# One-hot products in place of a reload: the first 128 rows of each expert's list in a three-layer kernel

## The chip, the cores and the metric

The kernel runs on one core of one Trainium2 chip. The metric is device time in microseconds (us) of one execution, from the first to the last instruction of that core and what the device needs around them. The engines are TensorE (PE, with its weight loads PEld), VectorE (DVE), ScalarE (ACT), GpSimd (POOL) and SyncE (SP); the two memories on the core are SBUF and PSUM (the accumulators of TensorE).

## The reference

Three layers follow each other. Cut to what matters:

```python
def _attn_ref(q, k, v):                      # B=4, H=8, S=576, D=64, blocks of 64 are causal
    scores = np.matmul(q, k.transpose(0, 1, 3, 2)) / np.sqrt(64)
    scores = np.where(block_i >= block_j, scores, -1e9)
    attn = softmax(scores)                   # rows, with 1e-9 in the divisor
    return np.matmul(attn, v)

def _moe_ref(x, w_skip, w_gate, w1, w2):     # x: 2304 tokens x 512, 8 experts, hidden 1024
    do_compute = x @ w_skip > 0              # the other tokens pass unchanged
    xc = x[do_compute]
    logits = xc @ w_gate
    e_idx = np.argmax(logits, axis=1)
    gate_w = softmax(logits)[e_idx]
    for e in range(8):
        h = np.maximum(xc[e_idx == e] @ w1[e], 0.0)
        y[e_idx == e] = gate_w * (h @ w2[e])
    out[do_compute] = xc + y

def _moe2_ref(x, w_in, w_out, alpha):        # 512 -> 2048 -> 512, weights in float64
    h = x @ w_in
    g = np.maximum(h, 0.0) + alpha * np.minimum(h, 0.0)
    return (g @ w_out).astype(np.float32)
```

What each expert computes on depends on the data, so the kernel has to make, on the chip, a list of the tokens of each expert (token number and gate weight) before it can fetch their rows.

## The kernel before

**Attention** (0 to 243 us). Sixteen pairs of heads, four pairs to a batch. Each pair loads q, k and v, transposes them (`tr`, L210), splits them in two parts (`split_qk`, L223 to L227), makes five strips of scores (`sc`, L247 to L253), takes row maxima on DVE (`row_max`, L260, L263), exponents on ACT (`expo`), transposes the strips (`ptr`, L296, L298 and L311), and multiplies by v (`pv`). `xout` writes the finished rows x to the DRAM tensor `xd`. A table of offsets (`OFF`) and the framework's scheduler set the order of these instructions until the last batch; from the last steps of batch 3 on (`tc.manual_schedule()`) instructions stand as the program writes them. All transposes and the small products of the routing share three PSUM buffers (pool `ps_m`, tag `m`).

**Routing**, once for each batch b, is spread over the batch's last pair and the pair behind it: `route`, `weigh_all` and `route2` make the logits, the expert of each token and the exponents of the gate; `route3` makes the rank of each token within its expert (`rank`, five columns of 128 tokens) and the one-hot `eq` (L468: 5x32 entries a row, rank equal to 0..31). `route4` picks, through `pick` (L476, 20 small products with `eq` as weights), the token numbers of the first 32 ranks of each expert and adds them into `sli`; `route5` (L487 to L521, a chain on DVE) computes the gate `g`, the list places `pi`, and picks the gate weights into `slg`. The first 32 tokens of every expert so need no list in DRAM: their numbers are in `sid` and two gathers (`xgs`, L601) fetch their rows.

**The list.** All other tokens go through DRAM: `send` scatters (token, gate) pairs of 8 bytes into `lst` by five indirect DMAs of POOL for each batch (L506). For batch 3, `sends[B - 1]()` stands behind `s_x(0)`, and its first scatter waits for ACT's second copy there (`last_exp`, L702). Then four loads (`load_list`, L684) bring ranks 32 to 159, 160 to 287, and so on, of all experts back into SBUF as `li[0]` to `li[3]`; they wait for the scatters.

**The seam and the experts** (243 to 414 us). PE runs 13 products on constants (`warm`, L64), the last batch's gate pick, four loads of counts into registers (`load_areg`, L693), the transposes of `xgs` (`s_x`, L701), and, for the first 32 tokens of every expert, `s_one` (L717), `s_ht` (L701) and `s_two` (L733). The tokens beyond 32 come in chunks of 128 rows: `level0(e)` issues the gather of expert e's first chunk on POOL (through `li[0]`, L601; three buffers), `extra(e, ...)` runs it under a branch on the expert's count, and each chunk gathers the one behind it. `both(E, 0)` holds experts 0 and 1 under one branch (L928): it is skipped as a whole when neither has more than 32 tokens, as in the profiled run. `extra(2)` (branch L808) is the first one whose rows PE transposes (L701, `xg`). Weights of the experts stream in by `load_w` on SP (L84), a few at a time; buffers come free when an expert is done.

**The last layer** (414 us to the end) decodes its float64 weights on DVE and multiplies on PE; DVE's part lasts until about 520 us, PE's to the end.

## Time and profile before

| quantity | value |
|---|---|
| median of 3 runs | 842.71 us (842.01 to 846.03) |
| the profiled execution | 841.73 us |
| its span, first to last instruction | 840.1 us |
| PE busy in the span | 785.9 us (94%) |
| DVE, ACT, POOL busy | 459.5, 298.7, 164.6 us |
| mean granted clock of TensorE | 0.98 |

The profiled execution lies 0.98 us under the median, and 1.6 us of it lie outside the span. The page's busy shares are means over stages with different limits; the rows further below are cut by stage. Times in rows are counted from the span's start. "idle before <-releaser" is the time in which the engine stood still ahead of that group, and what the profile takes for the thing that ended it; "issue" means nothing that it shows. An engine name with a q behind it is the engine's sequencer (branches, register loads, waits).

### The profile page before, as it was taken

What the parts mean: (1) busy time and instruction counts of PE and PEld (TensorE: products, weight loads), DVE (VectorE), ACT (ScalarE), POOL (GpSimd) and SP (SyncE); (2) the same over time, 40 slices, a digit from 0 to 9 for tenths busy, and PEclk for the clock granted to TensorE, in tenths of its full rate; (3) what the DMA queues carried; (4) which work ended last, traced back from release to release, by engine and by line L of the source; (5) the groups of instructions that cost most, each with busy time, mean ns of one, the idle gap of its engine ahead of it and who ended that gap; (6) DMA issues with size and microseconds to landing.
All of it is one profiled execution on the core that took longest, in us unless ns stands there. A gap on an engine that the chain in (4) does not pass through costs nothing.

```text
span 840.1 us, 14547 instructions
## 1 busy us (share of the span) xinstructions
PE 785.9 (94%) x5553; PEld 609.5 (73%) x5553; DVE 459.5 (55%) x953; ACT 298.7 (36%) x779; POOL 164.6 (20%) x208
## 2 busy tenths in 40 slices
PE   8999999999976899897699888999999999999998
PEld 5777777777745567664588666888888888888897
DVE  5758567667549299990489898322322332222232
ACT  5776776776722122112243333211121112011211
POOL 1000200101113114213122122222222222222122
PEclk9999999999998999999799999999999999999999
DMA  7874545663317997816622230100110001000100
GB/s 142 201 207 111 139 93 132 120 167 80 95 42 210 311 305 247 315 59 203 211 94 89 76 105 22 51 0 1 51 51 1 1 26 51 0 1 1 47 5 25
DMA packets 96117, 85.77 MB, mean 102 GB/s; under 512 B 68601, under 2 KB 73913, under 8 KB 96016
## 3 DMA queue, kind: packets, MB, share of 16 engines
q1 hardware_dynamic: 92000, 77.54, 32.1%
q0 software_dynamic: 2816, 6.65, 2.5%
q8 instruction: 56, 0.92, 0.5%
q10 hardware_dynamic: 1200, 0.30, 0.2%
q14 instruction: 45, 0.37, 0.1%
HBM read 73.20 MB, written 11.71 MB: 101 GB/s over the span
## 4 chain that ended last, share of the span: by engine, by line
PE 39%; DVE 9%; issue 2%; ACT 1%; DVEq 0%; ACTq 0%
PE psf L1009 18%; PE psa L1040 6%; PE psa L1041 6%; PE psa L1050 6%; DVE dt L652 2%; DVE dr L656 1%; DVE gt L1022 1%; DVE dt L653 1%; DVE dr L654 1%; DVE dr L650 1%; DVE wkg L640 1%; DVE dt L649 1%; DVE dt L651 1%; PE psx L997 1%; DVE wlo L640 1%
## 5 line engine op out<-in xcount | busy, mean ns | idle before, releaser
L1009 PE MATMUL psf<-xs,whi 128*128 128x512 f32 (+1 forms) x640 | 158.0, 369 | 0.7 <-ACT xs L871 0.7
L1026 POOL TENSOR_TENSOR gl<-gt,gh 128x512 fp32r<-128x512 f32 (+1 forms) x80 | 96.4, 1205 | 316.2 <-ACT gh L1025 184.6
L1025 ACT ACTIVATE gh<-gt 128x512 fp32r<-128x512 f32 (+1 forms) x80 | 47.1, 589 | 263.6 <-PE psa L1041 137.8
L1009 PEld LDWEIGHTS psf<-xs,whi 128*128 128x128 f32 x640 | 114.5, 188 | 23.0 <-ACT xs L871 0.9
L1021 DVE TENSOR_SCALAR gu<-psf,alf 128x512 f32<-128x512 f32 (+1 forms) x64 | 43.7, 682 | 157.8 <-PE psf L1009 157.7
L1009 PE MATMUL psf<-xs,wlo 128*128 128x512 f32 (+1 forms) x320 | 79.3, 369 | 0.0
L277 ACT ACTIVATE pe<-pss,mx 128x512 f32<-128x512 f32 (+3 forms) x128 | 66.7, 526 | 13.6 <-DVE mx L260 12.1
L1009 PEld LDWEIGHTS psf<-xs,wlo 128*128 128x128 f32 x320 | 56.8, 188 | 10.3
L1040 PE MATMUL psa<-whi,gh 128*128 128x512 f32 x144 | 57.3, 398 | 6.8 <-ACT gh L1025 6.8
L285 ACT ACTIVATE pt<-pspt 128x512 f32<-128x512 f32 (+3 forms) x112 | 51.8, 488 | 30.7 <-PE pspt L311 30.0
L1040 PE MATMUL psa<-wkg,gh 128*128 128x512 f32 x144 | 57.0, 396 | 1.6 <-ACT gh L1025 1.6
L260 DVE TENSOR_REDUCE mx<-pss 128x2 f32<-128x1024 f32 (+1 forms) x64 | 52.3, 818 | 10.9 <-PE pss L249 10.7
L1022 DVE SCALAR_TENSOR_TENSOR gt<-psf,gu 128x512 f32<-128x512 f32 (+1 forms) x80 | 51.0, 637 | 11.6 <-POOL gl L1026 5.0
L1041 PE MATMUL psa<-wlo,gh 128*128 128x512 f32 x144 | 56.2, 390 | 0.0
L1041 PE MATMUL psa<-wkg,gh 128*128 128x512 f32 x144 | 56.2, 390 | 0.0
L311 PE MATMUL pspt<-ident,pe 128*128 128x128 f32 x320 | 51.0, 286 | 0.5 <-ACT pt L397 0.3
L336 PE MATMUL pso<-pt,vr 128*64 128x256 f32 (+1 forms) x384 | 47.1, 352 | 3.7 <-ACT pt L285 3.6
L872 DVE TENSOR_TENSOR xs<-psx,xs 128x512 fp32r<-128x512 f32 x18 | 12.5, 692 | 57.4 <-ACT xs L871 57.4
L336 PEld LDWEIGHTS pso<-pt,vr 128*64 128x64 f32 x384 | 29.8, 136 | 18.0 <-ACT pt L285 8.4
L766 PEld LDWEIGHTS psh<-xT,w1t 128*128 128x128 f32 x320 | 39.9, 207 | 1.9 <-issue 1.0
L766 PE MATMUL psh<-xT,w1t 128*128 128x128 f32 x320 | 40.7, 292 | 0.1
L311 PEld LDWEIGHTS pspt<-ident,pe 128*128 128x128 f32 x320 | 33.6, 141 | 7.5 <-issue 2.2
(233 smaller groups left out, 1351.6 us busy)
## 6 DMA issues: line engine op xcount, KB each, us to landing
w1t<-in_moe_w_dram SPq DMA_DIRECT2D x32, 512.0 KB, 6.1
w2t<-in_moe_w_dram SPq DMA_DIRECT2D x32, 512.0 KB, 5.3
dr<-in_moe_w_in_dram SPq DMA_DIRECT2D x16, 512.0 KB, 5.8
dr<-in_moe_w_out_dram SPq DMA_DIRECT2D x16, 512.0 KB, 3.6
out_dram<-ob SPq DMA_DIRECT2D x18, 256.0 KB, 2.0
qr<-in_q_dram SPq DMA_DIRECT2D x32, 128.0 KB, 4.0
vr<-in_v_dram SPq DMA_DIRECT2D x32, 128.0 KB, 2.6
kr<-in_k_dram SPq DMA_DIRECT2D x30, 128.0 KB, 4.7
```

What stands on the lines that cost most here:

```text
L260: nc.vector.tensor_reduce(out=m, in_=ps[:, :, 0:128 * i + 128], axis=AX.X, op=ALU.max, negate=True)
L277: ins = nc.scalar.activation(out=pt[:, x, 0:n], in_=ps[:, x, 0:n], func=AF.Exp, bias=m[:, x:x + 1], scale=1.0, accum_out=d["sum"][:, x * 4 ...
L285: nc.scalar.activation(out=o, in_=a, func=AF.Copy)
L311: nc.tensor.transpose(ps[:, y, j, :], e[:, x, j * 128:j * 128 + 128], ident)
L336: nc.tensor.matmul(d["o"][hs, c0:c0 + n * 128], v5[:, j, x, :], pt[:, x, 2 * j:2 * j + n].rearrange("p n c -> p (n c)"), start=(j == 0), s ...
L766: nc.tensor.matmul(ps[:, f], w[:, kk, c:c + 128], self.xT[:, kk], start=(kk == 0), stop=(kk == 3))
L1009: nc.tensor.matmul(ps[:, 0:n], wsp[f // 4 * 4 + kk][a][:, ws], c[:, kk, 0:n], start=(n0 == 0 and kk == 0), stop=(n0 == 2 and kk == 3))
L1022: nc.vector.scalar_tensor_tensor(out=t[:, 0:n], in0=ps[:, 0:n], scalar=0.0, in1=u[:, 0:n], op0=ALU.max, op1=ALU.add)
L1026: nc.gpsimd.tensor_tensor(out=lo[:, 0:n], in0=t[:, 0:n], in1=hi[:, 0:n].bitcast(F32), op=ALU.subtract)
L1040: nc.tensor.matmul(o, hi[:, ts], whi, start=(f == 0), stop=False)
L1041: nc.tensor.matmul(o, hi[:, ts], wlo, start=False, stop=False)
L1050: nc.tensor.matmul(acc[w, t], lo[:, t * 128:t * 128 + 128], whi, start=False, stop=False)
```

## The change

For the first 128 list rows of each expert (ranks 32 to 159, what `li[0]` held) the list is made in SBUF in the way that the first 32 ranks already are. `first_eq` makes a second one-hot `eqf` (5x128 entries a row: rank equal to 32..159); `first_pick` multiplies it with `ohi` (token numbers) and later with `ohg` (gates), five products each, and adds the result on DVE into `fli` and `flg`. For batches 0 to 2 this runs inside `route4` and `route5`, in the attention. For the last batch the token pick stands behind the two `xgs` gathers and ahead of `route5`. The tile `first` takes the place of `li[0]`, one list load is gone, and `level0(0)` to `level0(2)` stand ahead of `sends[B - 1]`, of the weight loads that are tied to it, and of the remaining three list loads.

```diff
+    iot32 = acst.tile([128, 128], BF16, name="iot32")
+    nc.vector.tensor_scalar(out=iot32, in0=iot, scalar1=32.0, scalar2=None, op0=ALU.add)
+    first = const.tile([128, E, 2], I32, name="first")
+    fli = acst.tile([128, E, 2], F32, name="fli")
+    nc.vector.memset(fli[:, :, 0], float(PADROW))
+    nc.vector.memset(fli[:, :, 1], 0.0)
+    flg = acst.tile([128, E, 3], F32, name="flg")
+    nc.vector.memset(flg, 0.0)
...
+    def first_eq(b):
+        eq = T5("eqf", 128, BF16)
+        nc.vector.tensor_tensor(out=eq, in0=iot32.unsqueeze(1).to_broadcast([128, 5, 128]), in1=rs[b][4].to_broadcast([128, 5, 128]), op=ALU.is_equal)
+        rs[b].append(eq)
+
+    def first_pick(b, src, n, acc):
+        ps = ps_m.tile([128, E, n], F32, tag="m", name="psl")
+        for t in range(5):
+            nc.tensor.matmul(ps, rs[b][6][:, t], src[:, t], start=(t == 0), stop=(t == 4))
+        nc.vector.tensor_tensor(out=acc, in0=acc, in1=ps, op=ALU.add)
+
+    def first_ids(b):
+        first_eq(b)
+        first_pick(b, rs[b][1], 2, fli)
+
     def route4(b):
         nc.vector.tensor_tensor(out=sli, in0=sli, in1=pick(b, rs[b][1], 2), op=ALU.add)
+        if b < B - 1:
+            first_ids(b)
...
         nc.vector.tensor_tensor(out=slg, in0=slg, in1=pick(b, ohg, 3), op=ALU.add)
+        first_pick(b, ohg, 3, flg)
...
     gather(xgs[1], sid[:, 1:2])
+    first_ids(B - 1)
+    nc.vector.tensor_tensor(out=first[:, :, 0], in0=fli[:, :, 0], in1=fli[:, :, 1], op=ALU.add)
     route5(B - 1)
+    nc.vector.tensor_reduce(out=first[:, :, 1].bitcast(F32), in_=flg, axis=AX.X, op=ALU.add)
...
-    li = [mw.tile([128, E, 2], I32, tag=f"li{i}", name="li", bufs=1) for i in range(KX)]
+    li = [first] + [mw.tile([128, E, 2], I32, tag=f"li{i}", name="li", bufs=1) for i in range(1, KX)]
...
     s_x(0)
-    sends[B - 1]()
-    tied[0] = last_exp[0]
-    load_w(2, range(4, 8))
-    for i in range(KX):
-        load_list(i)
...
-    level0(0)
-    level0(1)
-    level0(2)
+    for e in range(3):
+        level0(e)
+    sends[B - 1]()
+    tied[0] = last_exp[0]
+    load_w(2, range(4, 8))
+    for i in range(1, KX):
+        load_list(i)
     s_one(0)
```

What that does to the order is shown at three places. A row is one instruction with its line, its output and inputs; line numbers of the kernel after are its own, some 8 to 30 higher. `x4` folds equal rows; "..." stands for further pairs of the same kind.

**The seam, PE.** Before, behind the last batch's token pick (`eq`, L476), the count product (L595) and the 13 products on `ones`, comes the gate pick:

```order
L476 MATMUL psl<-ohi,eq 32x4
L595 LDWEIGHTS ones
L595 MATMUL psl<-run_cnt,ones 128x8
L64 MATMUL psw<-ones 128x512
...
L476 LDWEIGHTS eq
L476 MATMUL psl<-ohg,eq 32x6
...
L693 TENSOR_LOAD cnt x4
L701 MATMUL pst<-ident,xgs 128x128 x4
```

After, in the same place:

```order
L484 MATMUL psl<-ohi,eq 32x4
L621 MATMUL psl<-run_cnt,ones 128x8
L64 MATMUL psw<-ones 128x512
...
L495 LDWEIGHTS eqf
L495 MATMUL psl<-ohi,eqf 128x16
...
L484 MATMUL psl<-ohg,eq 32x6
...
L495 MATMUL psl<-ohg,eqf 128x24
...
L722 TENSOR_LOAD cnt x4
L730 MATMUL pst<-ident,xgs 128x128 x4
```

Five products for the token numbers now stand behind the 13 on `ones`, and five for the gates behind the gate pick.

**The seam, DVE.** Before, `route5`'s chain follows the counts at once:

```order
L590 TENSOR_TENSOR sid<-sli 128x2
L592 CAST sidf<-sid 128x1
L596 CAST cnt<-psl 128x8
L598 TENSOR_TENSOR cnt<-cnt 128x1 x2
L487 TENSOR_REDUCE g<-ex 128x5
L488 TENSOR_SCALAR g<-g 128x5
```

After:

```order
L616 TENSOR_TENSOR sid<-sli 128x2
L618 CAST sidf<-sid 128x1
L622 CAST cnt<-psl 128x8
L624 TENSOR_TENSOR cnt<-cnt 128x1 x2
L489 TENSOR_TENSOR eqf<-iot_113,rank 128x640
L496 TENSOR_TENSOR fli<-fli,psl 128x16
L638 TENSOR_TENSOR first<-fli 128x8
L512 TENSOR_REDUCE g<-ex 128x5
```

The addition into `fli` reads PE's five products, and all of `route5`'s chain stands behind it.

**The seam, POOL.** Before, the scatters of batch 3 stand ahead of the gathers through `li` (a one-element memset, `pad`, stands between every two):

```order
L601 DMA xgs<-xd,sid 128x512
L693 TENSOR_LOAD cnt x4
L506 DMA lst<-pr,pi 19456x2
...
L69 MEMSET pad 1x1
L601 DMA xg<-xd,li 128x512
```

After:

```order
L627 DMA xgs<-xd,sid 128x512
L722 TENSOR_LOAD cnt x4
L69 MEMSET pad 1x1
L627 DMA xg<-xd,first 128x512
...
L531 DMA lst<-pr,pi 19456x2
```

Three gathers moved ahead of five scatters, and they read `first` in place of a loaded list.

**The attention, PE, first batch** (batches 1 and 2 have the same pattern). Before, behind the token pick, the transposes of a finished strip (L296) and the next strip of scores (L247, 128x384):

```order
L476 MATMUL psl<-ohi,eq 32x4
L296 MATMUL pspt<-ident,p_1304 128x128 x4
L247 MATMUL pss<-kh,qh 128x384
L298 MATMUL pspt<-ident,p_1304 64x128
L247 MATMUL pss<-kh,qh 128x384
```

After:

```order
L484 MATMUL psl<-ohi,eq 32x4
L495 LDWEIGHTS eqf
L495 MATMUL psl<-ohi,eqf 128x16
...
L255 MATMUL pss<-kh,qh 128x384 x2
L255 MATMUL pss<-kl,qh 128x384
L304 MATMUL pspt<-ident,p_1312 128x128 x4
```

The scheduler put the five products behind the pick and set the transposes behind three products of the next strip.

**The attention, DVE, the same place.** Before, `eq` is followed by small steps of `route5` and the next pair's `tid`, and the row maxima `m` and `mx` stand among them:

```order
L468 TENSOR_TENSOR eq<-iot,rank 128x160
L496 TENSOR_REDUCE po<-ob 128x5
L513 CAST tg<-pr 128x5
...
L263 TENSOR_REDUCE m_1285<-pss 128x1
...
L520 TENSOR_TENSOR ohg<-ohb,tg 128x120
L260 TENSOR_REDUCE mx<-pss 128x2
L225 SCALAR_TENSOR_TENSOR ql<-psq,qh 128x512
```

After:

```order
L476 TENSOR_TENSOR eq<-iot,rank 128x160
L489 TENSOR_TENSOR eqf<-iot_113,rank 128x640
L271 TENSOR_REDUCE m_1293<-pss 128x1
L521 TENSOR_REDUCE po<-ob 128x5
...
L268 TENSOR_REDUCE mx<-pss 128x2
L233 SCALAR_TENSOR_TENSOR ql<-psq,qh 128x512
L295 COPY xt<-pso 128x512
L503 TENSOR_TENSOR sli<-sli,psl 128x4
L496 TENSOR_TENSOR fli<-fli,psl 128x16
```

The 640-entry comparison stands ahead of both row maxima and of `ql`; the addition into `fli` stands behind `sli`'s.

## Rows read from the trace of the kernel before

**Rows 1.** Windows by stage: PE, PEld, DVE, ACT, POOL busy, PEclk, DMA share, GB/s

```profile
16.00:243.00 227.00, 219.47 (x2136) 161.57 (x2134) 148.22 (x429) 158.47 (x499) 18.60 (x38) 1.00 0.54 130
243.00:269.00 26.00, 15.99 (x272) 10.53 (x268) 19.66 (x49) 5.08 (x16) 10.41 (x18) 0.90 0.58 142
269.00:413.95 144.95, 123.35 (x1063) 86.57 (x1064) 99.94 (x156) 30.15 (x76) 33.90 (x37) 0.91 0.72 245
```

**Rows 2.** Timeline of the seam, PE: start, duration, what [idle before <-releaser]

```profile
243.04 2.96 PE L64 MATMUL psw<-ones 128*128 128x512 bf16 x13
246.79 0.41 PE L476 MATMUL psl<-ohg,eq 128*32 128x6 bf16 x20 [0.79 <-DVE ohg L520]
248.83 0.63 PE L701 MATMUL pst<-ident,xgs 128*128 128x128 f32 x4 [1.62 <-issue]
...
262.34 0.44 PE L701 MATMUL pst<-ident,sh 128*128 128x128 f32 x2
269.07 1.09 PE L701 MATMUL pst<-ident,xg 128*128 128x128 f32 x4 [6.29 <-DMA xg<-xd,li]
```

**Rows 3.** Line L928, 255 to 275 us: ns min/median/max, first and last start

```profile
L928 PEldq COMPARE_BRANCH  x1: 5240/5240/5240, 261.6 to 261.6; - x1
```

**Rows 4.** Line L823 at 280 to 295 us, another branch of the experts

```profile
L823 PEldq COMPARE_BRANCH  x2: 3045/4048/5052, 281.6 to 287.1; - x2
```

**Rows 5.** Line L693, loads of counts into registers, 246 to 269 us

```profile
L693 PEldq TENSOR_LOAD <-cnt x10: 300/306/494, 246.9 to 267.9; - x10
```

**Rows 6.** Timeline of the seam, POOL and DMA issues of SP

```profile
250.22 1.02 POOL L506 DMA_INDIRECT lst<-pr,pi  x1 [4.20 <-ACT xts L702]
259.46 2.25 SPq L684 DMA_DIRECT2D li<-lst  x4
262.38 0.98 POOL L601 DMA_INDIRECT xg<-xd,li  x1 [5.91 <-DMA li<-lst]
264.93 0.94 POOL L601 DMA_INDIRECT xg<-xd,li  x1 [0.23 <-issue]
```

**Rows 7.** Tile xg, 264.5 to 269 us: from the last two issues to landing

```profile
DMA to landing us min/median/max: 4.0/4.2/4.3
```

**Rows 8.** Timeline of the seam, DVE

```profile
243.91 0.18 DVE L487 TENSOR_REDUCE g<-ex 128x5 f32<-128x40 f32 x1
246.46 0.28 DVE L520 TENSOR_TENSOR ohg<-ohb,tg 128x120 bf16<-128x120 bf16 x1
```

**Rows 9.** DVE groups by shape, 70 to 90 us: total us, mean ns | idle before

```profile
L468 DVE TENSOR_TENSOR eq<-iot,rank 128x160 bf16<-128x160 bf16 x1 | 0.3, 318 | 0.0
L458 DVE TENSOR_TENSOR ohi<-ohb,tid 128x80 bf16<-128x80 bf16 x1 | 0.2, 204 | 0.0
```

**Rows 10.** Timeline, PE, 237 us: ten products of the last batch's routing

```profile
237.44 1.19 PE L420 MATMUL psl<-wbd,xt 128*128 128x18 f32 x10
```

**Rows 11.** Windows of the seam, columns as in rows 1

```profile
246.00:249.00 3.00, 0.58 (x23) 0.52 (x23) 1.04 (x7) 0.00 (x0) 0.01 (x1) 1.00 0.37 134
250.34:253.75 3.41, 3.41 (x40) 2.13 (x36) 1.57 (x3) 0.39 (x1) 2.96 (x5) 0.50 0.82 216
```

**Rows 12.** Timeline of the first batch's routing, PE, 80 to 82 us

```profile
80.17 0.41 PE L476 MATMUL psl<-ohi,eq 128*32 128x4 bf16 x20
80.51 0.66 PE L296 MATMUL pspt<-ident,p 128*128 128x128 f32 x4
...
81.81 0.61 PE L247 MATMUL pss<-kl,qh 64*128 64x384 f32 x2
```

**Rows 13.** The same stretch, DVE

```profile
79.71 1.22 DVE L260 TENSOR_REDUCE mx<-pss 128x2 f32<-128x1024 f32 x1
80.85 0.68 DVE L225 SCALAR_TENSOR_TENSOR ql<-psq,qh 128x512 fp32r<-128x512 f32 x1
```

**Rows 14.** Timeline of the start, DVE's first work on data

```profile
6.37 0.69 DVE L225 SCALAR_TENSOR_TENSOR ql<-psq,qh 128x512 fp32r<-128x512 f32 x1 [2.31 <-ACT qh L223]
```

**Rows 15.** Waits of SP's queue: released by, total us, times, longest

```profile
SPq L84 <- PE psy L799: 26.1, 1, 26.1
```

## The prediction made before the run

> **What bounds the kernel now.** I read the windows by stage first, then the timeline of TensorE (PE) at the seam, then the lines on which it stands still there. By stage, PE is busy 219.5 of 227 us in the attention and 123.4 of 145 us among the experts, and only 16.0 of 26 us at the seam [rows 1]. So in the attention nearly every us that is given to PE, or that PE has to wait, is a us of the kernel, and at the seam there are about 10 us to win.
>
> The largest hole of the seam is 6.29 us, from 262.78 (the transposes of `sh` end) to 269.07 (those of `xg` start); the profile names the gather of `xg` as what ended it [rows 2]. That is the hole at which the change aims: the gather needs `li[0]`, `li[0]` needs the scatters, and it all runs in a row from 250.22 to 264.93 [rows 6]. But in the hole PE's sequencer has a branch of its own. The one over experts 0 and 1 (L928) starts at 261.6 and takes 5.24 us, so it ends at 266.84 [rows 3]. Behind it stand three loads of counts at 0.31 us each, some 0.1 us apart, to about 268.1 [rows 5], and the next branch. The gather of expert 2, the third, is issued at 264.93 and lands 4.0 us later, at 268.93 [rows 6, 7]. So without any wait for the gather PE would start at about 268.4 in place of 269.07: **the gather holds PE for 0.6 us, not for 6.3**. The label names whatever came last. It is no peculiarity of this place: other branches of the experts took 3.05 and 5.05 us with no list load near [rows 4].
>
> What the row shows is a branch of 5.24 us in PE's sequencer. [...]
>
> **The change part by part.** *What it takes away at the seam.* The gather's 0.6 us: the new gathers are issued some 12 us earlier, ahead of the scatters. [...] The other branches are the bounds, 3.05 to 5.05 us against 5.24 [rows 3, 4]: a gain between 0 and 2.2 us. [...] Sum: -1.1 us (-0.6 to -2.8).
>
> *What it adds at the seam.* Before, `route5`'s chain on DVE starts at 243.91, beside the 13 products on `ones` (PE until 246.00), and its last step `ohg` ends at 246.74; PE picks at 246.79 [rows 2, 8]. After, `eqf` comes first. Its 640 entries cost, by the slope between 80 and 160 entries (204 and 318 ns), about 1.0 us; from 243.9, where `g` starts now, it is done by 245.0 [rows 8, 9]. That is hidden. But the five products that read it stand in PE's order behind the 13 on `ones`, so they start at 246.0. Their price lies between a quarter of the pick's 20 (0.1 us [rows 2]) and half of ten products with whole columns (0.6 us [rows 10]); I take 0.3. Then DVE adds `fli`, makes `first` (0.18 us each, as for `g` [rows 8], with a handover), and only then starts `route5`: at about 246.8 in place of 243.91, +2.9 us (2.7 to 3.3). Everything on PE behind the gate pick moves with it: the pick itself (to 249.7), the register loads, the transposes of `xgs`, `s_one`, `s_two`, the branch. The five gate products behind the pick add 0.1 to 0.6 more; with part of that under the register loads' start I take 0.1. So **+3.0 us (2.8 to 3.9)**.
>
> Queued behind the waiting addition on DVE are, besides `route5`, `gat` and the weights' decoding. On POOL the three gathers (1.3 us apart [rows 6]) fill 4 us that were idle: the first scatter had waited 4.20 us for ACT's copy of `xts` [rows 6], and will wait for the same copy, 3 us later. If that cover were gone, the scatters would move another 1 us, and the list loads with them; nothing on PE would feel it, since the first chunk behind needs `li[1]` only after the branch. SP's list loads, three in place of four, go from 259.46 to about 262.5; the loads of later experts' weights, tied to PE's progress, move by the net shift of PE.
>
> *TensorE's clock.* The `s_one` products ran at half clock, 3.41 us from 250.34 to 253.75, behind 3 us in which PE was busy 0.58 us [rows 11]. The change makes that quiet stretch about 3 us longer. The stretch at 0.50 would have lasted half as long at full clock: 1.7 us lost. Twice that, or none, are the bounds, -1.7 to +1.7; a longer rest speaks for more, I take +0.5.
>
> *The attention, three times.* PE gets ten more small products per batch: five times 0.02 to 0.12 us, twice, 0.2 to 1.2 us [rows 10, 12]; I take 0.6. DVE gets about 1.0 us for `eqf` and two additions of about 0.18. Before, DVE has `mx` from 79.71 and `ql` from 80.85 to 81.53, and PE starts the transposes L296 at 80.51, right behind the pick [rows 12, 13]. After, `eqf` stands ahead of both row maxima and of `ql`, while `ohg` (0.28) has gone behind: `ql` ends about 0.5 us later, at 82.0. Two buffers (`sli`'s and `fli`'s products) are now held out of the three in `ps_m` and `psq` holds the third until `ql` is done, so the transposes can't start before 82.0. PE has the five products and three strip products in front (two took 0.61 [rows 12], so about 0.2 to 0.3 each), to 81.4: a stall of 0.6, and some more where the fifth transpose waits for `sli`'s addition. The second pick, of the gates, comes late enough to be covered. Together 0.6 + 0.8 = **+1.4 us per batch, +4.2 for three**. Bounds: 0.2 per batch if the scheduler's other order swallows all but the cheapest products; 2.0 if `mx`'s delay reaches the exponents too: 0.6 to 6.0.
>
> *At nothing:* the new constants at the start, since DVE then waits 2.31 us for its first data [rows 14]; a few tenths of work.
>
> *Does the shift reach the end?* PE carries it through the experts, where each transpose, product and branch follows the last on PE. Weights have slack: SP once waited 26.1 us for PE to give back a buffer [rows 15]. At 414 us the last layer starts behind PE's last `s_two`. So it passes one to one.
>
> **Sum** against the profiled 841.73 us: -1.1 + 3.0 + 0.5 + 4.2 = +6.6, so 848.3. That run lies 0.98 under the median of 842.71; as a change of the median it is 849.3 us. About 0.5% (4.2 us) is what a measurement of this kernel can tell from no change: under 838.5 is faster, over 846.9 slower.
>
> **The rivals.** (a) *The hole is the gather's after all*, and the branch only waits along. For it: the profile's own label. Against it: the branch's 5.24 us and those at places without a gather. Then -6.3 in place of -1.1: 849.3 - 5.2 = 844.1 us, no change; with the attention at its low end, 840.5. It decides if PE's branch shows under 1 us in the new run. (b) *The attention takes it for almost nothing*: the scheduler's order is only an order, and at 7.5 us of idle PE in 227 there is some give. With 0.4 per batch, the cheap products alone, 849.3 - 3.0 = 846.3: no change. [...] (d) *Both delays grow*: the attention's stall at its 2.0 per batch and the seam's half clock doubled: 849.3 + 1.8 + 1.2 = 852.3. (e) *(a) and (b) together*: 841.1; to be faster by over 0.5% it would need no loss in the seam too, with the `ones` products giving way: 838.1.
>
> **How the numbers follow.** Chances: the forecast with (c) and (d) 0.66, (a) 0.12, (b) 0.17, (e) 0.05. The forecast and (d) lie above 846.9, but for a small part of their lower edge; (a), (b) and most of (e) lie within 0.5%. So slower 0.63, same 0.32, faster 0.05. The range from 844.5 to 852.5 takes in (b), (c), (d) and half of (a), and leaves out some 2 in 10.
>
> **What would show it.** In the new profile: (1) PE's branch at the seam still takes 3 to 5.3 us, and PE's idle time ahead of the `xg` transposes is still over 4 us, now put down to the branch or to "issue"; (2) the gather of expert 2 lands some 14 us before that; (3) `g` starts near 246.8, the gate pick near 249.7; (4) the attention ends some 4 us later, with waits of the L304 transposes on `ql`. Wrong would be: an idle stretch of under 1 us ahead of `xg` (then (a)), an attention that ends within 1 us of 243 (then (b)), or an expert stage that is shorter although PE starts it later.

## The result, and the profile after

The changed kernel takes 852.17 us (median of four runs, 851.74 to 854.97) beside 844.37 us for the kernel before (four runs, 842.01 to 846.40): **1.010 times the time, 95% interval 1.0061 to 1.014**, so 5 to 12 us slower. The forecast was +6.6 us and 849.3 us; by the medians the change measures +7.8 us (the kernel before had 842.71 us in its first three runs, and 844.37 with a fourth). The profiled run of the changed kernel took 852.08 us (span 850.4), 10.35 us more than the profiled run before (841.73).

To see where they come from I cut both traces at the same events on TensorE (PE) and subtracted stage by stage. "Attention" runs from the first batch's token pick to the last batch's; then come the seam (to the transposes of `xgs`), the shared experts (to the first transposes of `xg`), the experts (to the first product with `xz`), the join (to the first `psf` product), and the last layer (to the end of PE's last product).

| us | before | after | difference | in the forecast |
|---|---|---|---|---|
| up to the first token pick | 80.17 | 79.91 | -0.26 | 0 |
| attention, three batches | 162.49 | 166.39 | +3.90 | +4.2 |
| seam: token pick to `xgs` | 6.18 | 8.77 | +2.59 | +3.0 |
| `xgs` to `xg` | 20.24 | 18.73 | -1.51 | -1.1 + 0.5 |
| experts | 148.28 | 148.83 | +0.55 | 0 |
| join | 6.42 | 6.81 | +0.39 | 0 |
| last layer | 412.51 | 417.02 | +4.51 | 0 |

The first four rows are about what the forecast said, 4.7 us in place of 6.6. The largest row is one that it doesn't have.

**The seam.** These windows of the trace after answer to [rows 1] (PE, PEld, DVE, ACT, POOL busy, PEclk, DMA share, GB/s):

```profile
16.00:246.65 230.65, 222.03 (x2164) 161.47 (x2163) 150.78 (x438) 159.26 (x499) 18.64 (x38) 1.00 0.49 128
246.65:273.80 27.15, 16.94 (x283) 10.96 (x279) 19.46 (x52) 5.19 (x16) 11.48 (x20) 0.87 0.49 131
273.80:422.60 148.80, 124.07 (x1126) 87.18 (x1126) 104.72 (x158) 29.83 (x76) 33.99 (x36) 0.91 0.72 243
```

PE is busy for about the same share of each stage as it was (96%, 62% and 83%, against 97%, 62% and 85%), and the middle one takes 27.15 us where it took 26.00. PE's timeline of the seam after, to be laid beside [rows 2]:

```profile
246.30 0.41 PE L484 MATMUL psl<-ohi,eq 128*32 128x4 bf16 x20 [0.24 <-DVE eq L476]
249.49 0.27 PE L495 MATMUL psl<-ohi,eqf 128*128 128x16 bf16 x5
253.04 0.43 PE L484 MATMUL psl<-ohg,eq 128*32 128x6 bf16 x20 [3.28 <-DVE ohg L545]
255.07 1.09 PE L730 MATMUL pst<-ident,xgs 128*128 128x128 f32 x4 [1.36 <-issue]
...
273.80 1.09 PE L730 MATMUL pst<-ident,xg 128*128 128x128 f32 x4 [4.41 <-DVE dt L678]
```

The five new products run behind the 13 on `ones`, at 249.49, and the gate pick then waits 3.28 us for `ohg`, where it waited 0.79. DVE after, beside [rows 8]:

```profile
247.56 0.81 DVE L489 TENSOR_TENSOR eqf<-iot,rank 128x640 bf16<-128x640 bf16 x1
249.80 0.17 DVE L496 TENSOR_TENSOR fli<-fli,psl 128x16 f32<-128x16 f32 x1 [1.43 <-PE psl L495]
250.09 0.19 DVE L512 TENSOR_REDUCE g<-ex 128x5 f32<-128x40 f32 x1
252.70 0.28 DVE L545 TENSOR_TENSOR ohg<-ohb,tg 128x120 bf16<-128x120 bf16 x1
```

`eqf` is done at 248.37, and then DVE stands still 1.43 us, until PE has come through the `ones` products to the five that `fli` needs. Only then does `g` start. Between the `sh` transposes and those of `xg` PE is still idle for 4.41 us. The gather can't be the reason any more. In the timeline of POOL after, the third gather is issued ahead of the first scatter of the lists:

```profile
253.42 0.95 POOL L627 DMA_INDIRECT xg<-xd,first  x1 [0.21 <-issue]
256.86 1.03 POOL L531 DMA_INDIRECT lst<-pr,pi  x1 [2.49 <-ACT xts L731]
```

The view of tile `xg` after, 249 to 259 us, gives the time from issue to landing of the three early gathers:

```profile
DMA to landing us min/median/max: 3.9/4.0/4.4
```

So the last is there by 257.8, 16 us before PE starts on `xg`.

What PE's sequencer does in that time is in the view of line L956 after, the branch that was L928 before [rows 3] (ns min/median/max, first and last start):

```profile
L956 PEldq COMPARE_BRANCH  x1: 3915/3915/3915, 268.2 to 268.2; - x1
```

It ends at 272.13; the loads of counts and the next branch (L837) follow, which ends at 273.63, and PE starts at 273.80. The releaser that the timeline names, a step of the decoding on DVE, writes nothing that the `xg` transposes read: with the gather gone from the end of the wait the label fell on something else that ended late.

TensorE's clock [rows 11] has a longer quiet stretch in front, 3.28 and 1.36 us of waiting on PE with the picks between, where it was 0.79 and 1.62 us. It is at the lower of its two levels (0.50) for longer, 4.83 us of the `xgs` transposes and the shared experts in place of 3.41:

```profile
255.07:259.90 4.83, 4.69 (x40) 2.72 (x44) 1.21 (x3) 0.77 (x2) 2.59 (x5) 0.50 0.68 196
```

**The attention.** The first batch's routing in the timeline of PE after, to be laid beside [rows 12]:

```profile
81.32 0.66 PE L304 MATMUL pspt<-ident,p 128*128 128x128 f32 x4 [0.23 <-DVE ql L233]
...
82.92 0.65 PE L368 MATMUL psx<-ident,xt 128*128 128x128 f32 x4
...
86.00 0.33 PE L255 MATMUL pss<-kh,qh 64*128 64x128 f32 x2 [0.40 <-ACT pe L285]
...
86.67 0.41 PE L484 MATMUL psl<-ohg,eq 128*32 128x6 bf16 x20
...
87.15 1.07 PE L319 MATMUL pspt<-ident,pe 128*128 128x128 f32 x8
```

The same in the timeline of PE before:

```profile
82.57 0.66 PE L360 MATMUL psx<-ident,xt 128*128 128x128 f32 x4
...
85.18 0.41 PE L476 MATMUL psl<-ohg,eq 128*32 128x6 bf16 x20
...
85.78 1.09 PE L311 MATMUL pspt<-ident,pe 128*128 128x128 f32 x8
```

On DVE, `ohg` before, and `ql` and `ohg` after, in the timelines of the two traces (`ql` before is in [rows 13]):

```profile
79.51 0.28 DVE L520 TENSOR_TENSOR ohg<-ohb,tg 128x120 bf16<-128x120 bf16 x1
```

```profile
80.59 0.68 DVE L233 SCALAR_TENSOR_TENSOR ql<-psq,qh 128x512 fp32r<-128x512 f32 x1
...
86.33 0.28 DVE L545 TENSOR_TENSOR ohg<-ohb,tg 128x120 bf16<-128x120 bf16 x1
```

After led by 0.26 us at the token pick. The L304 transposes now wait for `ql`, as forecast, and start 0.81 us later than L296 did [rows 12], so 1.07 us are lost there, of which some comes back in the next products: at the transposes of `xt` (L368, before L360) the kernel after is 0.61 us behind with the lead counted. `ql` itself isn't later: it ends 1.36 us behind the token pick in both kernels. The second loss is at the gate pick: before, `ohg` was done ahead of the token pick; after, it ends at 86.61, and the gate pick comes right behind it, and behind a wait of 0.40 us for an exponent, at 86.67 in place of 85.18. The next transposes start at 87.15 in place of 85.78, 1.63 us behind with the lead counted. Of what each batch loses 1.3 us are left, in each of the three.

**The last layer.** The longest pieces of the chain that ended last (start, us, what) lie there, one group of twelve products behind the other. One of the kernel before:

```profile
524.58 2.75 PE psf L1009 x12
```

The first of the list after:

```profile
530.27 2.80 PE psf L1037 x12
```

No instruction of it was changed. Its `psf` products are 1.6% slower: 232.95 ns from one to the next in place of 229.17, over all that follow each other without a wait. Its `psa` products, which begin later, lose half as much by the same measure: 229.6 ns in place of 227.7. Together that is most of the 4.5 us.

### The profile page after: what moved, and what is told of

Read it like the earlier page. It is cut to its first block, busy times and chain, and to the rows that moved or that the text cites. A ratio compares the mean times of both kernels' runs of the same rounds, so it can differ in the third digit from the quotient of the medians.

```text
span 850.4 us, 14642 instructions
## 1 busy us (share of the span) xinstructions
PE 792.2 (93%) x5593; PEld 609.1 (72%) x5593; DVE 467.0 (55%) x971; ACT 299.4 (35%) x779; POOL 166.0 (20%) x208
## 4 chain that ended last, share of the span: by engine, by line
PE 39%; DVE 10%; issue 2%; ACT 1%; DMA 0%; DVEq 0%; ACTq 0%
PE psf L1037 18%; PE psa L1068 6%; PE psa L1069 6%; PE psa L1078 6%; DVE dt L681 2%; DVE dr L685 1%; DVE gt L1050 1%; DVE dt L682 1%; DVE dr L683 1%; PE psy L762 1%; DVE dr L679 1%; DVE wkg L669 1%; DVE dt L678 1%; DVE dt L680 1%; PE psx L1025 1%
## 5 line engine op out<-in xcount | busy, mean ns | idle before, releaser
L1037 PE MATMUL psf<-xs,whi 128*128 128x512 f32 (+1 forms) x640 | 160.4, 373 | 0.7 <-ACT xs L899 0.7
L795 PEld LDWEIGHTS psh<-xT,w1t 128*128 128x128 f32 x320 | 37.4, 196 | 1.9 <-issue 1.0
L1078 PE MATMUL psa<-wkg,gl 128*128 128x512 f32 x140 | 38.4, 391 | 0.0
```

Source lines behind the costliest of these rows:

```text
L1037: nc.tensor.matmul(ps[:, 0:n], wsp[f // 4 * 4 + kk][a][:, ws], c[:, kk, 0:n], start=(n0 == 0 and kk == 0), stop=(n0 == 2 and kk == 3))
L1078: nc.tensor.matmul(acc[w, t], lo[:, t * 128:t * 128 + 128], whi, start=False, stop=False)
```

## The experiments

Two questions came first: what slows the untouched last layer, and whether attention, seam and hole cost what the forecast says for the reasons that it gives. A third came out of the traces: why the experts take longer.

### The same kernels again

Both kernels were run again unchanged.

> The kernel before, unchanged, as a yardstick on the same chip as the next three. In the old trace twelve products of the last layer (L1009) took 2.75 us, in the trace of after 2.80 us, and that alone is 4.5 us between 527 us and the end. Theory P (the place of the tiles in SBUF sets the pace): 2.75 us here again, a time near 842. Theory C (the pace belongs to the chip or to the execution): here it is what the other three kernels of this batch show too.

> The kernel after, unchanged. Theory P: twelve products of the last layer take 2.80 us, time near 852, 9 to 10 us over before on this chip. Theory C: the same pace as the kernel before on this chip, and a difference of about 5.7 us, what the two traces differ by at 424 us. The late experts' branch that took 7.68 us in the trace of after (L837): near 7.7 us again if the code's place sets it, between 4 and 8 us if it is chance.

> The kernel after, unchanged, beside e14 on the same chip. By its two earlier traces: 8.8 us from the last token pick to the xgs transposes, 18.7 to 18.8 to the xg transposes, 149 to 153 us for the experts, 417.0 us for the last layer. If those differ here by over 1 us up to the xg transposes, the chip or the execution sets them; if they repeat, the program does.

Before again took 844.69 us, in one run. After again took 855.55 against 844.04, ratio 1.0105 (1.0048 to 1.0161); a third time, on another chip, 862.95 against 849.42, ratio 1.017 (1.0136 to 1.0205). Some stages repeat to 0.1 us: the seam (8.78 and 8.78; before 6.20) and the last layer (417.05 and 417.02; before 412.48). The attention does so on most chips (166.34; before 162.53), but took 168.3 on that of the third run, chip 0. Others don't. From `xgs` to `xg` it was 18.80 and then 22.86, the experts took 153.4 and 153.0 where the first trace has 148.8, and the kernel before took 150.1. **So the pair of profiled runs flatters the change among the experts**, and one pair of traces can't price that stage.

### The place of the tiles: e3, e4, e5, e14

The change adds `first`, 64 bytes per partition, to the pool of constants, and all tiles behind it move by 64 bytes, `xs` and the weights of the last layer with them. In e3 the kernel before gets an unused tile of that size, in e4 the changed kernel one more; in e5 three small tiles of the changed kernel share one and an unused list tile is kept, so that the last layer's tiles lie where they were before. e14 is e5 again, beside e13.

The edit of e3:

```diff
-    nc.vector.memset(fill, PADROW)
+    nc.vector.memset(fill, PADROW); const.tile([128, 16], F32, name="gap")
```

That of e5 and e14:

```diff
-    sid = const.tile([128, 2], I32, name="sid")
+    small = const.tile([128, 8], I32, name="small"); sid = small[:, 0:2]
...
-    sidf = const.tile([128, 1], F32, name="sidf")
+    sidf = small[:, 2:3].bitcast(F32)
...
-    gat = const.tile([128, 2], F32, name="gat")
+    gat = small[:, 4:6].bitcast(F32)
...
-    li = [first] + [mw.tile([128, E, 2], I32, tag=f"li{i}", name="li", bufs=1) for i in range(1, KX)]
+    li = [first] + [mw.tile([128, E, 2], I32, tag=f"li{i}", name="li", bufs=1) for i in range(KX)][1:]
```

> The kernel before with 64 unused bytes per partition in the pool of constants, where the change puts its list: every later tile on that side lies 64 bytes higher, no instruction differs. Theory P: the last layer's twelve products go from 2.75 to 2.80 us and the kernel is 4 to 5 us slower than before (ratio 1.005 to 1.006). Theory C: the same time and the same pace as before on this chip (within 1 us).

> The kernel after with 64 more unused bytes behind its list, so that those tiles lie 128 bytes higher than before in all. Theory P: the pace is back at 2.75 us if the place counts modulo 128 bytes, and the time is 4 to 5 us under that of after (about 847.5); still 2.80 us if any shift does it. Theory C: no difference from after (within 1 us).

> The kernel after, with three small constant tiles (sid, sidf, gat) put into one and one unused list tile kept, so that all weights, x and result tiles of the last layer lie at the same SBUF addresses as in the kernel before; the instructions and their order are those of after. Theory P (64 bytes of shift set the pace of the last layer): twelve of its products take 2.75 us as in before, 424 us to the end lasts 412.5 us and not 417, and the kernel is 4.5 us faster than after: some 847 to 849, about 5 us over before. If the pace comes from the added instructions instead: 2.80 us, no gain over after.

> The kernel of e5 again, beside after. Theory S (e5's loss of 3.6 us between the xgs and the xg transposes and of several us among the experts comes with its program): 22 us and 154 to 156 us again, and slower than e13 in spite of the faster last layer. Theory X (it came with that chip or that execution): 18.7 us and about 150 us here, and a time 4 to 5 us under e13's.

From the chain that ended last in e3, the kernel before with the gap:

```profile
520.35 2.80 PE psf L1009 x12
```

And in e14, the changed kernel without the shift:

```profile
537.66 2.75 PE psf L1037 x12
```

The pace goes with the place of the tiles, in either kernel: last layer 417.05 us in e3, 412.51 in e5 and 412.50 in e14. With 128 bytes (e4) it is 416.20, at 233.56 ns a `psf` product, so twice the shift doesn't bring the old pace back. e4 as a whole took 853.24 us, 1.0097 times the kernel before (1.0065 to 1.0129), as the changed kernel does. In time e3 is 1.0067 times the kernel before (1.0039 to 1.0096): 64 unused bytes cost about 5.7 us, in which the 4.5 us fit. e14, on the same chip as e13, took 854.88 against 862.95 us, and is 1.0065 times the kernel before (1.0042 to 1.0088) where e13 is 1.017.

In e5 the time did not follow: 859.19 us, ratio 1.0155 (1.0107 to 1.0203), though its last layer did take 412.51. Its other stages took the gain: `xgs` to `xg` 22.40 and the experts 156.25. e14 has the former too (22.71), and so has the unchanged e13 beside it (22.86), so it isn't the shift that is undone that does it. It goes with the chip: all eight traces taken on chip 0 (e5 to e8, e13 to e16) have 21.3 to 26.6 us in this stage, and the others 17.6 to 20.3, but for three in which a gather came late (e11, e17, e18). In six of the eight PE waits 1.8 to 5.5 us for ACT's second copy of `sh`, which it doesn't on other chips; what holds ACT there is open. So is how far one batch of runs can be trusted: e5 and e14 are the same kernel on the same chip, and their ratios, 1.0155 and 1.0065, have intervals that don't meet. In the other two of the eight PE itself stops. e16 (below) has the instructions of e9, and between its first shared products PE stands still again and again for nothing that the profile shows, where e9 has none of that. One row of PE's timeline in e16:

```profile
260.04 1.12 PE L751 MATMUL psh<-w1t,xts 128*32 128x256 f32 x3 [0.64 <-issue]
```

### The attention: e6, e11, e12, e15

e6 is e5 without the early picks of the first three batches, whose rows are then missing from the list; e11 is the kernel before with those alone, their results unread; e12 is the changed kernel with the comparison `eqf` of these batches, but not the products and additions, so that the same rows are missing; in e15 token ids and gates of a batch are picked by one set of five products with 40 columns, on top of e5.

The edit of e6:

```diff
-        if b < B - 1:
+        if b < -1:
             first_ids(b)
...
-        first_pick(b, ohg, 3, flg)
+        if b == B - 1: first_pick(b, ohg, 3, flg)
```

That of e12:

```diff
         if b < B - 1:
-            first_ids(b)
+            first_eq(b)
...
-        first_pick(b, ohg, 3, flg)
+        if b == B - 1: first_pick(b, ohg, 3, flg)
```

In e11 the kernel before has the change's constants but `first`, `first_eq`, `first_pick` and `first_ids`, and these lines:

```diff
+        if b < B - 1:
+            first_ids(b)
...
+        if b < B - 1: first_pick(b, ohg, 3, flg)
```

The core of e15:

```diff
+        ohc = sm.tile([128, 5, E, 5], BF16, tag="ohi", name="ohc", bufs=2)
+        ohi = ohc[:, :, :, 0:2]
...
-        first_pick(b, ohg, 3, flg)
+        first_pick(b, rs[b][6], 5, flc)
```

> e5 without the comparisons, products and additions for batches 0 to 2 (their tokens of ranks 32 to 159 are then missing from the list made on chip). Forecast's theory: the last batch's token pick starts at 242.6 to 243 again, 3.65 us earlier than in after, a time of 843 to 845. Rival (the scheduler's order shifts for another reason, or DVE's work elsewhere): it stays above 245.

> The kernel before with the attention part of the change alone: comparisons, products and additions of batches 0 to 2, whose results nothing reads; list loads, gathers and the seam as before, last layer's tiles at their old addresses. Forecast's theory: first token pick to last token pick takes 166.3 us as in after (before: 162.5), the last layer 412.5 us, the seam as in before. If the attention's loss came from something else in the program, 162.5 us.

> The kernel after with the comparison of batches 0 to 2 kept and their ten products and two additions a batch left out (the rows of these batches are missing from the list made on chip). Forecast put 0.6 us a batch on the products and 0.8 on the stall that DVE's delay and the held PSUM buffers make. If PE's stall on the buffers is the larger part, the stretch from first to last token pick falls to 163 to 164 us; if DVE's 0.81 us comparison is the cost, it stays at 165 to 166 us.

> A version meant to keep the early gathers and give back what the change costs: addresses of the last layer as in before; token and gate picks of the 128 rows in one product of 40 columns per block, behind the gate pick (5 products, one buffer and one addition a batch in place of 10, 2 and 2); the last batch's comparison right behind the smaller one. Expected: first to last token pick 164 to 165 us (after 166.4, before 162.5), seam 6.3 to 6.8, last layer 412.5; with 18 and 150 us for the rest some 844, near the kernel before. If S holds for every program with these addresses: 3 to 8 us more.

The attention took 162.44 us in e6, 166.35 in e11, 163.89 in e12 (in all 852.19, 852.51 and 849.31 us, one run each). So the part costs 3.9 us, alone as with the rest (4.5 between e5 and e6, on chip 0), 1.4 of it by the comparison and 2.5 by products, additions and the buffers that they hold. With the latter gone (e12), PE's waits for `ql` and for the exponent are gone too. Half as many products (e15) gave a little back: from one token pick to the next 58.77 and 58.59 us, where the other traces of chip 0 with the change have 59.1 (after 58.9, before 57.6). In all the attention took 168.23 in e15, as in e13 and e14 (168.32, 168.31), but these three traces alone have a granted clock of 0.61 to 0.92 between 205 and 215 us, where all others have 1.00, and the comparison of the totals says nothing. How the 2.5 us divide among products, additions, buffers and the order that the scheduler gives them, no run here shows. e15 as a whole took 853.73 us where 844 was expected, ratio 1.005 (1.0021 to 1.0078), the lowest of the timed versions with the change, and over the kernel before.

### The seam: e9 and e16

e9 takes the wait at the seam away: the last batch's comparison stands at the head of `route4` and its five products ahead of the 13 on `ones`; the additions stand behind `ohg`. e16 is the same with e5's places of the tiles.

```diff
     def route4(b):
+        if b == B - 1: first_eq(b)
...
+    fps = ps_m.tile([128, E, 2], F32, tag="m", name="psl")
+    for t in range(5):
+        nc.tensor.matmul(fps, rs[B - 1][6][:, t], rs[B - 1][1][:, t], start=(t == 0), stop=(t == 4))
     warm(ps_s, "s", 13)
...
-    first_ids(B - 1)
-    nc.vector.tensor_tensor(out=first[:, :, 0], in0=fli[:, :, 0], in1=fli[:, :, 1], op=ALU.add)
     route5(B - 1)
```

> The kernel after with the last batch's part reordered: its 640-entry comparison right behind the 160-entry one, its five token products ahead of the 13 products on ones, and the two additions behind the gate chain's last step. Forecast's theory (the gate chain stands 2.6 us later at the seam only because it waits for products that wait for the 13): from the token pick to the xgs transposes 6.7 to 7.1 us in place of 8.78 (before: 6.18), some 1.8 us off the seam. Rival (DVE's added work itself is the delay): it stays over 8 us.

> e9 (the last batch's products ahead of the 13 on ones) with e5's addresses. Expected from e9 and e5: 166.4 us to the last token pick, 6.3 us to the xgs transposes, 412.5 us for the last layer; to the xg transposes 17.6 us as in e9 if theory X holds, about 21 if S does.

PE's timeline in e9:

```profile
250.74 0.41 PE L484 MATMUL psl<-ohg,eq 128*32 128x6 bf16 x20 [0.43 <-DVE ohg L546]
...
252.78 0.63 PE L735 MATMUL pst<-ident,xgs 128*128 128x128 f32 x4 [1.40 <-issue]
...
270.37 1.09 PE L735 MATMUL pst<-ident,xg 128*128 128x128 f32 x4 [5.34 <-DVE wlo L674]
```

The wait for `ohg` is 0.43 us in place of 3.28 and the seam 6.31 us in place of 8.78: it was the order, DVE behind five products behind 13. The granted clock stayed at 1.00 too, and the first 64 shared products took 3.66 us in place of 5.47. `xg` starts 17.60 us after `xgs`, with a hole of 5.34 us, and the branch in it took 4.9 us. One run of e9 took 850.53 us, one of e16 857.71; e16 has the seam (6.32) and the last layer (412.52), and loses 7.7 us between `xgs` and `xg` (25.31), where it has the gaps shown above.

### The hole: e7, e8, e10

e7 is the kernel before, and e8 is e5, without the branch over experts 0 and 1 and the code under it. Neither expert has more than 32 tokens in this data, so nothing that is computed changes. e10 is the changed kernel without the list loads; its later chunks then move nothing of use.

The edit of e7 and e8:

```diff
-    both(E, 0)
+    nxt.pop(0), nxt.pop(1)
```

That of e10:

```diff
     for i in range(1, KX):
-        load_list(i)
+        nc.vector.memset(li[i], PADROW)
```

> The kernel before without the branch over experts 0 and 1 and the code under it (which the data skip: both have fewer than 33 tokens). Forecast's theory, two things that each hold PE: PE's register loads end near 264, but the gather lands at about 268.9 all the same, so the hole ahead of the xg transposes stays at 5.5 to 6.3 us and the time gains at most 0.6 us by it. If the branch were no cost: the same hole too. If the branch alone were the cost (gather not needed so late): a hole of 1 to 2 us.

> e5 without the same branch. Here the gather has landed some 15 us ahead. Forecast's theory: the hole of 4.40 us ahead of the xg transposes shrinks to 1.0 to 1.7 us (three register loads at 0.4 us each), 2.7 to 3.4 us off the seam, so that 'with the branch gone' early gathers would pay. Rival (something else than the branch holds PE, such as weights or ACT's copies): the hole stays over 3 us.

> The kernel after without the three list loads; their tiles are filled with the number of the padding row instead, so that later chunks gather and scatter nothing of use. Taken away: some 3000 packets of 8 bytes between 266 and 272 us, while the sequencers fetch code. Theory F (the fetches of code compete with these packets): PE's branch at the seam goes from 3.9 to about 3 us, and the stretch from the xgs to the xg transposes from 18.7 to about 17.8 us. Rival (the branch takes what it takes): 3.9 us and 18.7 us again.

In this stage it gave nothing: `xgs` to `xg` took 21.42 us in e7 against 20.24, and 22.29 in e8 against 22.40 in e5 (in all 844.98 us, as the kernel before beside it with 845.04, and 851.01, under e5's 859.19; one run each). But the hole went. In e8 the `xg` transposes come in two halves, and PE waits 0.29 and 0.57 us ahead of them, where e5 has 4.00 us and 1.0 to 1.7 were expected. What that gained was lost earlier in the stage, in the wait for ACT's second copy of `sh`, 5.50 us in place of 1.83. PE's timeline in e8:

```profile
268.24 0.69 PE L730 MATMUL pst<-ident,sh 128*128 128x128 f32 x2 [5.50 <-ACT sh L748]
...
277.83 0.41 PE L730 MATMUL pst<-ident,xg 128*128 128x128 f32 x2 [0.29 <-DMA xg<-xd,li]
```

In e7, where 5.5 to 6.3 us were expected, PE waits 0.80 and 2.13 us ahead of the two halves, the second time for ACT:

```profile
272.70 0.44 PE L701 MATMUL pst<-ident,xg 128*128 128x128 f32 x2 [2.13 <-ACT hts L702]
```

It too waits for ACT's copy of `sh` before (2.54 us). Both runs also move all code behind the branch, and both are of chip 0, so what the branch is worth in time they don't show. That it makes the hole, the traces with it show plainly. In all twelve that have it together with the early gathers (after, e2, e4 to e6, e9, e10, e12 to e16) the hole is as long as that branch plus 0.48 to 0.54 us, with branches of 3.5 to 4.9 us and holes of 4.0 to 5.3, and `xg` starts 0.16 or 0.17 us behind the end of the next branch.

In e10, without the list loads, the branch took 3.9 us, and PE's timeline has the same hole, 4.40 us:

```profile
274.41 0.69 PE L730 MATMUL pst<-ident,xg 128*128 128x128 f32 x4 [4.40 <-issue]
```

So the list loads don't slow the branch (853.69 us in all), and theory F falls. In the trace after, between 266 and 272 us, the queue with the list loads (q1) moved 3120 packets, 0.02 MB in all, and the two that the page lists as `instruction` (q8 and q14) two each.

e11 shows the other side. It has the lists and gathers of the kernel before. The `xg` transposes in its timeline of PE:

```profile
276.40 1.08 PE L726 MATMUL pst<-ident,xg 128*128 128x128 f32 x4 [9.41 <-DMA xg<-xd,li]
```

The issue of the third gather, on POOL:

```profile
270.83 0.95 POOL L626 DMA_INDIRECT xg<-xd,li  x1 [0.22 <-issue]
```

And the branch, by its line:

```profile
L953 PEldq COMPARE_BRANCH  x1: 4089/4089/4089, 265.8 to 265.8; - x1
```

The branch was over at 269.9. The gather, issued at 270.83, wasn't in until 276.3, and the hole is 9.41 us: here more than half of it *is* the gather's. From the token pick to the landing it takes 26.3 us in the trace before and 29.3 in e11. So both chains reach PE, and which is last, and by how much, depends on the run. Counted from 0.17 us behind the end of the next branch, the old gather held PE for 0.56 us in the trace before, 0.60 in e1, 0.23 in e3, 1.89 in e18, 4.83 in e11 and 8.04 in e17 (e17 and e18 are told below). That is what the early gathers are worth, by estimate, beside each.

### The place of PE's program: e17, e18

Between 280 and 430 us the kernels before and after have the same branches in the same order, and they don't take the same time. The late passes of the two lines in question in the trace before, by line:

```profile
L818 PEldq COMPARE_BRANCH  x1: 330/330/330, 371.1 to 371.1; - x1
L808 PEldq COMPARE_BRANCH  x1: 4840/4840/4840, 391.1 to 391.1; - x1
```

The same after (L847 was L818, L837 was L808):

```profile
L847 PEldq COMPARE_BRANCH  x1: 3756/3756/3756, 370.4 to 370.4; - x1
L847 PEldq COMPARE_BRANCH  x1: 3511/3511/3511, 382.5 to 382.5; - x1
L837 PEldq COMPARE_BRANCH  x1: 7682/7682/7682, 392.6 to 392.6; - x1
```

What the last one does to PE, in the timeline before:

```profile
396.06 2.24 PE L733 MATMUL psy<-w2t,hts 128*32 128x128 f32 x52 [3.55 <-PEq L808]
400.72 1.07 PE L733 MATMUL psy<-w2t,hts 128*32 128x128 f32 x12 [2.42 <-issue]
```

And after:

```profile
400.42 0.66 PE L762 MATMUL psy<-w2t,hts 128*32 128x128 f32 x8 [6.39 <-PEq L837]
404.34 1.08 PE L762 MATMUL psy<-w2t,hts 128*32 128x128 f32 x16 [3.26 <-issue]
```

It is so each time: the last pass of L808 or L837 took 4.84, 5.25 and 5.44 us in the three traces with PE's program of before (before, e1, e3), and 6.7 to 7.7 us in the nine with that of the change or e9's (after, e2, e4, e5, e9, e10, e13, e14, e16), which also have the two late passes at 3.3 to 3.8 us. Kernels with 10, 20 or 30 of the change's products on PE (e6 and e12, e15, e11) have one such pass each, and 6.5 to 8.7 us at the last. In the pair of profiled runs this is covered up by a wait that only the trace before has, in its timeline of PE:

```profile
343.22 1.09 PE L701 MATMUL pst<-ident,xg 128*128 128x128 f32 x4 [2.96 <-DMA xg<-xd,li]
```

At the same place after:

```profile
343.65 0.63 PE L730 MATMUL pst<-ident,xg 128*128 128x128 f32 x4
```

That gain isn't the change's own: e3, with the gathers of before, has no such wait (its experts took 144.06 us), and e5, with those of the change, waits 3.67 us.

The change adds 40 products to PE's program, 80 instructions with their loads of weights. In e17 the kernel before gets just that: the 13 products on `ones` at the seam are cut into 53 short ones, and no other instruction moves. In e18 there are 128 more, 256 instructions.

The edit of e17:

```diff
-    warm(ps_s, "s", 13)
+    warm(ps_s, "s", 53, 120)
```

That of e18 (the last argument, which e17 and e18 add to `warm`, is a product's columns):

```diff
-                    warm(ps_s, "s", gaps[fn])
+                    warm(ps_s, "s", gaps[fn] * 6 + (gaps[fn] == 8), 84)
...
-    warm(ps_s, "s", 13)
+    warm(ps_s, "s", 80, 80)
```

> The kernel before, with the 13 products of 512 columns on `ones` behind the first token pick of the last batch cut into 53 products of 120 columns. No other engine's order changes, nothing else of PE's; behind this place every PE instruction stands 80 instructions later in PE's program, about as the 40 products of the change set it, and the tiles of the last layer stay where they were. Theory A, the place of a branch's target in PE's program sets how long the branch waits for its code: the branch over the last expert's rows (L808), 4.84, 5.25 and 5.44 us in three traces of the kernel before, takes 6.5 to 7.7 us, as in the traces with the change (L837: 6.7 to 7.7), and the branch on L818, which never took more than 0.1 us there, takes 3.3 to 3.9 us as L847 does with the change; the experts' stage is 1 to 5 us longer than the 144 to 150 us of before, and the time some 2 to 5 us over the kernel before. Rival B, the branch waits for other traffic that the change brings: L808 stays between 4.8 and 5.5 us, L818 under 0.1, and the time within 2 us of the kernel before. The last layer takes 412.5 us by both.

> The kernel before, with 128 more products on `ones` in the same stretches (8, 4 and 13 products of 512 columns become 49 of 84, 24 of 84 and 80 of 80), so that PE's program behind the seam stands 256 instructions later, which at 64 bytes each are 16 KB, the size of one packet on PE's instruction queue in these traces (60 packets, 0.98 MB). Theory A: shifted by one whole packet, the targets stand as they did against the packets, so L808 is back at 4.8 to 5.5 us and L818 under 0.1 us, unlike in the run with 40 more products. Rival A', the branches only get slower with a longer program: L808 over 6.5 us here too. Rival B expects 4.8 to 5.5 us and under 0.1 us as for 40 more. Time: by A within 2 us of the kernel before, if the shorter products cover DVE's work as the longer ones did (the gate pick not later than 0.5 us).

(L818 does take long once in the kernel before: 4.26 us at 307.9. The expectation speaks of its late passes, and those took 0.33 and 0.28 us, not under 0.1.) The same lines in e17:

```profile
L818 PEldq COMPARE_BRANCH  x1: 3291/3291/3291, 374.2 to 374.2; - x1
L818 PEldq COMPARE_BRANCH  x1: 3251/3251/3251, 386.5 to 386.5; - x1
L808 PEldq COMPARE_BRANCH  x1: 7282/7282/7282, 396.8 to 396.8; - x1
```

And in e18:

```profile
L818 PEldq COMPARE_BRANCH  x1: 330/330/330, 368.5 to 368.5; - x1
L808 PEldq COMPARE_BRANCH  x1: 5944/5944/5944, 388.5 to 388.5; - x1
```

40 products with no other change give the pattern of the changed kernel, the same late passes waiting about as long; 128 give back that of the kernel before (5.94 us is 0.5 over the highest seen there). Even the branch at the seam goes along: 3.96 us in e17, as after (3.92), and 5.02 in e18, as before (5.24), though not without exception (4.9 in e9). e7 and e8, without the code under that branch, turn the pattern both ways: e7, made from the kernel before, has late passes of 3.40 and 3.28 us and a last one of 6.03, and e8 has 0.34, 0.28 and 4.48, where e5 has 3.29, 3.65 and 7.13. The experts took 148.07 us in e8 and 156.25 in e5. In time e17 is 849.30 us against 845.68, **1.0044 (1.0023 to 1.0065)**, and e18 845.56, 1.0001 (0.9974 to 1.0028). More code by itself can't be told from no change; its place can, in this batch of runs. That is theory A, and rivals A' and B fall. What moves meanwhile the traces before and after show: in each of their 14 branches of PE over 2 us (2.96 to 7.68 us) one or two packets of 16 KB start on the queue that the page lists as `q8 instruction`, two of them in the 5.24 us of the branch at the seam before. From 540 to 816 us PE runs 2579 products and loads of weights before and 2505 after, and this queue moves 10 and 9 packets, so by estimate one to some 258 and 278 of PE's instructions. Over the whole run it moves 56 before, 57 in e18 and 60 in e17, as after. By that estimate 256 instructions more put each target about where it was against the packets, and 80 don't, and the two runs agree. That PE waits for such a packet, no trace here shows by itself.

The two profiled runs lie further apart than the medians, 850.79 and 841.50 us, and some of that is at the seam. The branch there ends early, but the gather came late again, as PE's timeline in e17 shows:

```profile
273.91 1.08 PE L701 MATMUL pst<-ident,xg 128*128 128x128 f32 x4 [12.50 <-DMA xg<-xd,li]
```

So not all of e17's time need be the late branches'. By stage: experts 152.46 us in e17 and 145.90 in e18; the last layer is 412.55 and 412.52 in both. Over all traces the experts took 144.1 to 150.1 us, 147.1 in the mean, in the four whose branches are those of before (before, e1, e3, e18), and 148.8 to 156.3, 152.0 in the mean, in the ten with those of the change (the nine and e17). As a price that difference is too high: the traces of e3 and e18 are of the shortest of eleven runs (842.04 us, median 849.89) and the second shortest of ten (841.50, median 845.56). The branches themselves don't hang on that choice: the two late passes and the last one take 5.5 to 6.6 us together in the four traces, and 13.8 to 15.3 in the ten.

## Where the prediction held, and the step that failed

The direction held, and 852.17 us lies in the range, 0.3 us under its upper end. That is in part luck: the forecast's own parts measured 4.7 us in place of 6.6, and two costs that it had put at nothing made up for it and more. Between the two traces it is +10.35 us, and in three timed comparisons 1.010 to 1.017 times the kernel before, which is 8 to 14 us. The four signs that the prediction named all showed (the third, `g` and the gate pick, later by the 3.6 us of the attention). In its order:

- **The hole is the branch's, not the gather's.** Right: the early gather left 4.41 us of idle PE, in twelve traces the hole is the branch's length plus half a us, and rival (a) is out. Too narrow was the price: the 0.6 us were the margin between two chains in one run, and the six traces with the old gathers show 0.2 to 8.0.
- **The branch gets 0.5 us shorter.** No run shows that term. The branch got 1.3 us shorter, and not by less traffic beside it: e10 has still less and 3.9 us; e17 has all the traffic of before and 3.96 us. The place of the code does it, as far as the runs tell (e9's 4.9 us doesn't fit). With the gather's 0.6 us that is the -1.9 us by which the hole shrank (6.29 to 4.41), against -1.1 forecast.
- **The seam, +3.0.** Measured +2.59, by the chain that was named; `eqf` took 0.81 us against an estimate of 1.0, `g` starts 3.79 us behind the token pick in place of 1.26, 2.5 us later where 2.9 was forecast. e9 takes the cause away, and the 2.5 us come back.
- **The clock, +0.5.** 4.69 us of work at the lower level in place of 3.41 lose 0.64 us more. e9, without the long wait, shows 1.00 throughout.
- **The attention, +4.2.** Measured +3.9, but not in the parts as priced. `ql` was to end 0.5 us later and the transposes were to stall for 0.6 us and more; `ql` ends as soon behind the token pick as before, and the stall is 0.23 us. That the gate pick is covered was wrong: it is late by 1.75 us with the lead counted, and part of that comes back later. Two errors of opposite sign made a good sum, which is luck.
- **The shift reaches the end one to one.** Right for the shift. But the sum had no term for what the change does to instructions that it doesn't touch, and *this is the step that failed*, twice. What it puts at nothing is the work of the new constants at the start; the last layer, the largest row above, has no term, and neither has the place of PE's code. The tile `first` moves the last layer's operands by 64 bytes: +4.5 us, steady in every run (e3 and e14 show it from both sides). The 40 products move PE's program by 80 instructions: among the experts two more late branches wait and the last one waits longer, +3.6 us in time (e17, in one batch of runs), of which the profiled pair shows 0.55, as the run before lost 2.96 us to a gather there.
- **Rivals.** (b), attention nearly free, is out (e6, e11), and (e) with it. (c), counted with the forecast in the chances, stands for a branch of 3.05 us at the seam [rows 4] and 847.6 us in all; the branch took 3.92. (d) names 852.3 us, next to the result, by another way: its stall of 2.0 us per batch was 1.3.

By the numbers of the runs the bill is: attention +3.9, seam +2.6, last layer +4.5, PE's code +3.6 (e17, by the medians; part of it may be the seam's), and against it what the early gathers give, 0.2 to 8.0 us as the old gather came in good time or late. No version tried with the change beats the kernel before. One with e9's seam, e5's tiles and 88 further short products, which with the change's 40 make the 128 of e18, wasn't tried; its attention alone would still cost 3.9 us.

What stays open: why 64 bytes change the pace of the products; what stretches `xgs` to `xg` from 18 to 22 or 25 us with the same instructions on chip 0 (e9 and e16, after and e13); what makes the attention's 2.5 us beside the comparison; and why the chain of the gathers takes 26 us in one run and 29 or more in another.

## What to carry to other kernels

Ahead of a change list what it moves without touching it: tiles behind a new tile of the same pool, and code behind new instructions on an engine that branches. Both are easy to test without the change, by an unused tile of the same size and by as many idle instructions, and both were as large here (4.5 and 3.6 us) as the costs that the diff shows (3.9 and 2.6). And where two chains end close together in a wait, the margin of one trace is no price for either: look at it in several runs.

## What the runs showed of the hardware

- The last layer's `psf` products of 512 columns follow each other in 229.17 ns, and in 232.95 with the tiles 64 bytes further on (233.56 at 128 bytes); its `psa` products in 227.7 and 229.6 (229.5 at 128 bytes). The layer takes 4.5 us longer in 412.
- A branch on PE takes 0.065 to 0.086 us, 0.19 to 0.35, or 1.8 to 8.7 us, over all twenty traces; which of them goes with the place of the code, as the late passes in e17 and e18 show; on the other four engines none took over 0.41 us. The first kind are the most (the median of L837's four passes after is 0.085 us).
- 80 instructions more on PE, in a stretch that waits anyway, made a kernel 0.44% slower (0.23% to 0.65%), 256 more made no difference that can be told (-0.26% to 0.28%).
